# Attention, routing and MoE items on one core: a lent PSUM bank, a third sum on VectorE, the last pair in another order, and three kinds of step a slot later

## The chip, the cores and the metric

The kernel runs on one core of a Trainium2 chip. The time is the device time of one launch in microseconds; the figure that counts is the median of some runs, and beside it stands one execution that the hardware profiler recorded. The core's engines are TensorE (PE in the rows, with its weight loads as PEld), VectorE (DVE), ScalarE (ACT), GpSimd (POOL) and SyncE (SP, which issues most transfers). PSUM, where TensorE puts its results, has eight banks.

## The reference, cut to what matters

Three layers follow one another: attention with a tanh cap, a gated MoE that sends each token to its best expert, and a soft MoE whose experts work on 4 slots each.

```python
# 4 batches, 12 heads, 448 tokens, head size 64
scores = cap * np.tanh(scale * (q @ k.T) / cap)
attn = np.exp(scores - max); attn /= attn.sum(-1) + 1e-9
x = attn @ v                            # to (1792 tokens, 768)

# gated MoE: 8 experts, 768 -> 1024 -> 768
e_idx = argmax(x @ w_gate + modality_bias[modality_id], 1)
gate_w = softmax(logits)[e_idx]
out[e_idx == e] = gate_w * (relu(x @ w1[e]) @ w2[e])

# soft MoE: 8 experts, 4 slots each
logits = out @ phi
slot_input = softmax(logits, over tokens).T @ out
slot_out[e] = relu(slot_input[e] @ w1[e]) @ w2[e]
return softmax(logits, over slots) @ slot_out
```

## The kernel before, in words

**What sets the order.** The schedule is written by hand: each engine runs its instructions in the order in which the code issues them, and only semaphores hold it back. So an instruction that waits holds all that stands behind it on its engine. The table P near the end of the file (lines 1468 to 1475) gives the slots of the later part; nothing is planned at run time.

**Attention** works on 24 pairs of heads, 6 for each batch (NP_), as a pipeline. In the loop over p, TensorE makes the scores of pair p in three pieces (scores1, scores2, scores3), adds the products with v of pair p-1 (pv, then the last small piece pv2), and turns and normalises pair p-2 (post2, post3). The 448 keys are 3 chunks of 128 and a rest of 64; the rests of the pair's two heads share one 128-row tile. ScalarE takes tanh and exp, VectorE splits q and k into high and low parts (split), adds the exponentials of the chunks (adds1, adds2, 128x896 each) and scales the results. The sums over keys come from TensorE in post2 (line 507): each term of `sums[p]` is a tile under a constant weight `onesel`, in four column blocks, and a further term under the gate's weights `wg` gives the MoE logits. A pair has three such terms, head 0, head 1 and the shared rest.

**Banks in attention.** The pool ps_s has the tags s (two banks), s1, s2 and s0, ps_o and ps_x have one bank each, and ps_m has one, with tag "sm". In "sm" lie r_ps (the sums, read by VectorE at line 110), rt_ps (their transpose), and everything of the routing: rank_ps, tab_ps, tabt_ps. Tag s0 is used once a pair, by the second head of chunk 2 (scores3).

**Routing** of a batch begins two pairs after its last pair. The list `later` holds its steps, and the loop pops one at two places of each pair, once after post2 and once after scores3: s0 (9 small VectorE steps, the best expert), s1 (rank_ps: two matmuls that count tokens ahead of each one, then four additions to `base` and one for `rk`), s2, s3. After the third batch route_first follows: the most frequent expert, its slot table a2f, the sums over it (tab_ps, 12 small matmuls, line 329), their turn (tabt_ps, line 336), the indices, the gather of 4 tiles of rows by GpSimd (line 470) and the first expert weights. The fourth batch is routed later, in the item A.

**The last pair** (p = 23, LAST) goes through the same loop body. Then item_start closes the pools of attention and opens those of the items; the first weights are split (wsplits), ScalarE scales the four gathered tiles (xscale with True, line 478), and the last products and post steps follow, with six pieces that transpose and split the gathered rows (xpreps, line 766) between them.

**The items.** An item is one expert over 4 tiles of 117 gathered tokens, in 16 slots of 9 accumulating matmuls (128x468, lines 822 to 824: high times high, low times high, high times low). Item A comes first, then items 0, 1 and 2. `std_slots` puts further work into the slots by P: "pa" and "pb" are the second layer's logits and transposes for one quarter of the hidden rows (l_ps, h_ps, and s_ps in the later items), "dq" and "wq" quarters of 256 columns that are turned into q_ps and copied by VectorE to dhT and wphi (line 813), "comb" the combine weights of the item before (c_ps, line 862, a transpose of mcur into a bank of the Turns pool, which q_ps also uses). "plan" in A holds the routing of the fourth batch. At the end of an item the rows of the next are scaled and turned (xp, xprep). A rarely taken branch lies between A and item 0 (line 1219); after item 2 come the closing slots and the soft MoE, about 405 to 499 us, which stream their weights.

Of the kernel before, what the change touches and what calls it, by code (L numbers as in the profile page):

```python
# [9 lines left out]
F32 = mybir.dt.float32  # L10
# [42 lines left out]
def attn_moe_softmoe(ctx, tc, qT, kT, vP, cap, modality, w_gate, mod_bias, w1, w2, w2t, phi, m2_w1, m2_w2, out):  # L53
# [18 lines left out]
    W = 117  # L72
# [247 lines left out]

    def slot_tables(n, cols, col, sp, pp):
# [12 lines left out]
        def turn():  # L334
            tp = pp.tile([W, 2, NTAB], F32, tag="sm", name="tabt_ps")
            nc.tensor.matmul(tp.rearrange("p a n -> p (a n)"), lhsT=hold["sb"], rhs=fold, start=True, stop=True)
            tables(tp[:, :, :n], n, col, sp)

        return [sums, turn]
# [17 lines left out]

    def route_first(sp, pp):

# [33 lines left out]

        return [s0, s1, rest] + slot_tables(NT, NC1, NA, sp, pp)

# [171 lines left out]
    def attention(a1, a1q, a2p, first, ps_s, ps_o, ps_x, ps_m, item_start):  # L567
# [65 lines left out]

        def pv(p):
            vt = raw[p][2]
            o = o_t[p] = ps_o.tile([128, S], F32, tag="o", name="o_ps")
            for c in range(NKC):
                for h in range(2):
                    hd = slice(HD * h, HD * h + HD)
                    nc.tensor.matmul(o[hd], lhsT=vt[:, c, hd], rhs=pt_t[p][:, c, h] if c < 2 else pt_m[p][:, 1 + h],  # L640
                                     start=(c == 0), stop=False)
# [10 lines left out]
        extra.update({5 + i: call(nc.vector.memset, xg[:, i], 0.0) for i in range(NT)})  # L652
        extra[9] = zero_c
        n2 = 0
        spl[0] = first_split
        later = []
        for p in range(NPAIR):
            if p + 2 < NPAIR:
                raw[p + 2] = load_qkv(a1, a1q, p + 2)
            if p >= 4 and p % 2 == 0 and n2 < NRING + 1:  # L660
                m2_load(n2)
                n2 += 1
            scores1(p)
            if p >= 1:
                pv(p - 1)
                adds2(p - 1)
            if p + 1 < NPAIR:
                split(p + 1)
            if p >= 2:
                post2(p - 2, a1, ps_x, ps_m)  # L670
            if later:
                later.pop(0)()
            if p >= 1:
# [8 lines left out]
            if p in extra:  # L682
                extra[p]()
            if later:
                later.pop(0)()
            if p >= 2 and (p - 2) % NP_ == NP_ - 1:
                b = (p - 2) // NP_
                rb = route_batch(b, a2p, ps_m)
                later += rb
                if b == NB1 - 1:  # L690
                    f = route_first(a2p, ps_m)
                    later[-2] = lambda: (rb[-2](), f[0]())
                    later += [f[1], lambda: (f[3](), f[2]()), lambda: (f[-1](), gather(NA, NB1 * S), weights_first()),
                              lambda: None, lambda: None]
                later.pop(0)()
        while later:
            later.pop(0)()
        assert n2 == NRING + 1 and a1.end <= UNIT * (NRINGA - 1)
        wsplits, xpreps = item_start()
        wsplits[0]()  # L700
        xscale(NA, True)
        pv(LAST)
        adds2(LAST)
        post2(LAST - 1, a1, ps_x, ps_m)
        wsplits[1]()
        for f in xpreps[:3]:
# [241 lines left out]
    def std_slots(first, last, ncol, col, it, final=False):  # L948
# [8 lines left out]
        prep_x = lambda k: call(xprep, k, ("x", "sm", "sm")[k % 3])  # L957
        if not last:
            for k in range(3, KD):
                at(HB - 1, prep_x(k))  # L960
# [39 lines left out]
        fd, fw = quarters("dacc", "dhT", False), quarters("wacc", "wphi", first)  # L1000
        if not first:
            at(0, call(post_a, NF - 1))
            at(p["la"], logits_a)
# [107 lines left out]
    def prologue(key, e, col, rows=None, further=True):  # L1111
# [8 lines left out]
        for j in range(NR2):  # L1120
            w2load(j, e)
        for k in range(KD):
            xprep(k, "xa"[k % 2])

    def attention_any_cap():

        with ExitStack() as st:
# [12 lines left out]
            for p in range(NPAIR):  # L1140
# [43 lines left out]
                if hp == NP_ - 1:  # L1184
                    for f in route_batch(b, gx, ps_m):
                        f()
                    if b == NB1 - 1:
                        for f in route_first(gx, ps_m):
                            f()
# [80 lines left out]
    with ExitStack() as st:  # L1270
# [199 lines left out]
    "A": {"T": [0, 0, 0, 0, 3, 3, 3, 3], "wm": 3, "wq": 5, "pa": [6, 6, 9, 9, 12, 12, 15], "pb": [6, 7, 9, 10, 12, 13, 15], "nt": [10, 12, 12, 12], "cur": 10, "xp": [14, 14,  # L1470
        14], "xs": [13, 13, 13, 13], "plan": [0, 1, 1, 2, 2, 3, 4, 5, 7, 8, 8, 8, 9], "pool": [2, 3, 4, 6, 7, 8, 10, 14, 15]},
    "B": {"la": 0, "lb": 0, "lc": 5, "dturn": 1, "dh": 4, "dq": 5, "T": [0, 0, 0, 0, 4, 4, 4, 4], "wm": 4, "wq": 5, "pa": [6, 6, 9, 9, 12, 12,
        15], "pb": [6, 7, 9, 10, 12, 13, 15], "N": [6, 6, 6, 9, 9, 9, 9, 12], "comb": 5, "gath": 0, "cur": 12, "xp": [13, 13, 13], "xs": [1, 4, 4, 12], "rest": [1, 3, 7,
        9], "pool": [4, 5]},
# [69 lines left out]
```

## Time and profile before

| | before |
|---|---|
| median of 3 runs | 511.52 us (510.08 to 512.67) |
| the profiled execution | 508.24 us, its span 506.5 us |
| PE busy | 459.2 us, 91% of the span |
| DVE, ACT, POOL busy | 276.3, 250.3, 68.6 us |
| moved by DMA | 124.98 MB, mean 247 GB/s |
| attention | 0 to about 206 us |
| item A | 208.4 to 257.9 us |
| items 0, 1, 2 | 257.9 to about 405 us |
| closing slots, soft MoE | about 405 to 499 us |

The profiled execution is read by its stages, since each has another limit. A view by stretches gives the busy time of each engine, TensorE's granted clock (1.00 is 2.4 GHz, 0.50 is 1.2 GHz) and the share of the DMA engines. A timeline gives each instruction with the idle time of its engine before it and what ended that. A view of waits adds up what an engine waited for, line by line.

### The profile page before, as it was taken

How to read it: one execution, taken by the hardware profiler on the slowest of the kernel's cores; microseconds unless marked ns; L12 is line 12 of the kernel's file. 1: busy time of each engine (PE TensorE's matmuls, PEld its weight loads, DVE VectorE, ACT ScalarE, POOL GpSimd, SP SyncE). 2: the span in 40 equal slices, each digit the busy share in tenths (PEclk: the TensorE clock that was granted, in tenths of full speed). 3: DMA queues.
4: the chain of work that ended last, by engine and by line, in shares of the span. 5: the costliest groups of instructions: out<-in, count | busy, mean ns of one | idle time of the engine just before them, and what ended most of it. 6: DMA issues, size and time to landing. Idle time of an engine off the chain costs nothing. (4 is left out here: it accounts for less than half of the span.)

```text
span 506.5 us, 10871 instructions
## 1 busy us (share of the span) xinstructions
PE 459.2 (91%) x4181; PEld 298.6 (59%) x4181; DVE 276.3 (55%) x710; ACT 250.3 (49%) x402; POOL 68.6 (14%) x141
## 2 busy tenths in 40 slices
PE   7999989999999978989988999899989979977672
PEld 4556555564655544668875888688868845521221
DVE  4779889788978884575752355235523322001323
ACT  4988868787788767433442344234432311100222
POOL 3000000000000004024331403140014003120000
PEclk8999999999999999999999999999999989995987
DMA  6356644744353408679959797979589899999997
GB/s 198 103 119 189 219 140 124 230 138 114 121 157 104 132 20 226 209 260 356 283 170 338 217 319 233 325 234 313 200 295 326 292 393 415 416 411 417 414 414 285
DMA packets 56151, 124.98 MB, mean 247 GB/s; under 512 B 9385, under 2 KB 25456, under 8 KB 56096
## 3 DMA queue, kind: packets, MB, share of 16 engines
q1 hardware_dynamic: 53696, 117.54, 67.6%
q0 software_dynamic: 2256, 6.71, 4.7%
q8 instruction: 34, 0.56, 0.4%
q14 instruction: 21, 0.17, 0.1%
q10 hardware_dynamic: 144, 0.00, 0.0%
HBM read 112.52 MB, written 11.71 MB: 245 GB/s over the span
## 5 line engine op out<-in xcount | busy, mean ns | idle before, releaser
L608 ACT ACTIVATE arena<-arena,capb 128x1792 f32<-128x1792 f32 (+1 forms) x48 | 77.0, 1604 | 1.6
L822 PE MATMUL acc_ps<-xh,wh 128*128 128x468 f32 x192 | 75.7, 394 | 1.4 <-DVEq L1219 1.3
L107 DVE TENSOR_TENSOR wl<-rw,wh 128x384 fp32r<-128x384 f32 x49 | 27.4, 559 | 87.4 <-ACT wh L775 76.1
L823 PE MATMUL acc_ps<-xl,wh 128*128 128x468 f32 x192 | 71.9, 375 | 0.0
L824 PE MATMUL acc_ps<-xh,wl 128*128 128x468 f32 x192 | 71.7, 374 | 0.0
L107 DVE TENSOR_TENSOR arena<-arena 128x896 f32<-128x896 f32 x48 | 52.2, 1088 | 24.5 <-ACT arena L608 22.4
L640 PE MATMUL o_ps<-arena 128*64 128x448 f32 x288 | 59.6, 548 | 1.1 <-issue 0.5
L775 ACT CAST wh<-rw 128x384 fp32r<-128x384 f32 x64 | 32.5, 508 | 52.3 <-PE acc_ps L823 32.3
L605 ACT ACTIVATE arena<-s_ps 128x448 f32<-128x448 f32 x96 | 46.8, 541 | 8.6 <-PE s_ps L577 8.6
L470 POOL DMA_INDIRECT xg<-x_dram,idx x16 | 17.4, 1091 | 205.7 <-PE s_ps L577 176.6
L822 PEld LDWEIGHTS acc_ps<-xh,wh 128*128 128x128 f32 x192 | 36.1, 188 | 7.3 <-ACTq L1219 1.5
L943 ACT ACTIVATE h<-acc_ps 128x468 f32<-128x468 f32 x32 | 18.0, 562 | 43.0 <-PE acc_ps L824 40.5
L824 PEld LDWEIGHTS acc_ps<-xh,wl 128*128 128x128 f32 x192 | 36.0, 188 | 4.7 <-DVE wl L107 0.2
L823 PEld LDWEIGHTS acc_ps<-xl,wh 128*128 128x128 f32 x192 | 36.3, 189 | 3.5
L640 PEld LDWEIGHTS o_ps<-arena 128*64 128x64 f32 x288 | 18.5, 136 | 31.3 <-issue 21.7
L577 PE MATMUL s_ps<-qh,kh 64*128 64x448 f32 x144 | 31.9, 439 | 1.3 <-ACT kh L730 0.9
L600 ACT ACTIVATE arena<-sl_ps 128x448 f32<-128x448 f32 x24 | 13.1, 544 | 28.8 <-PE sl_ps L577 25.6
L577 PE MATMUL s_ps<-qh,kl 64*128 64x448 f32 x144 | 26.7, 366 | 0.1
L577 PE MATMUL s_ps<-ql,kh 64*128 64x448 f32 x144 | 26.7, 366 | 0.0
L107 POOL TENSOR_TENSOR wl<-rw,wh 128x384 fp32r<-128x384 f32 x15 | 15.4, 1026 | 75.6 <-ACT wh L775 41.2
L871 POOL DMA_INDIRECT c_dram<-cw,icur x16 | 17.5, 1094 | 51.1 <-DVE cw L107 34.4
L577 PEld LDWEIGHTS s_ps<-qh,kh 64*128 64x128 f32 x144 | 13.7, 187 | 17.1 <-ACT arena L605 8.5
(271 smaller groups left out, 759.0 us busy)
## 6 DMA issues: line engine op xcount, KB each, us to landing
ring<-in_moe_w_dram SPq DMA_DIRECT2D x30, 768.0 KB
w2r<-in_moe_w2t_dram SPq DMA_DIRECT2D x32, 384.0 KB
w2r<-in_moe_w_dram SPq DMA_DIRECT2D x28, 384.0 KB
arena<-in_moe_w_dram SPq DMA_DIRECT2D x13, 768.0 KB
rw<-in_moe_w_dram SPq DMA_DIRECT2D x24, 384.0 KB
arena<-in_moe_w_dram SPq DMA_DIRECT2D x22, 384.0 KB
arena<-in_v_dram SPq DMA_DIRECT2D x24, 256.0 KB
kr<-in_k_dram SPq DMA_DIRECT2D x23, 256.0 KB
```

The costliest lines, as they stand in the source:

```text
L107: (eng or nc.vector).tensor_tensor(out=out, in0=in0, in1=in1, op=op)
L470: nc.gpsimd.indirect_dma_start(out=xg[:, i, :], out_offset=None, in_=x_dram if rows is None else x_dram[:rows], in_offset=bass.IndirectOff ...
L577: nc.tensor.matmul(o, lhsT=kk[r, k], rhs=qq[r], start=(t == 0), stop=(t == 2))
L605: nc.scalar.activation(out=dst[:, h], in_=ps[h], func=AF.Tanh)
L608: nc.scalar.activation(out=t, in_=t, func=AF.Exp, scale=capb)
L640: nc.tensor.matmul(o[hd], lhsT=vt[:, c, hd], rhs=pt_t[p][:, c, h] if c < 2 else pt_m[p][:, 1 + h], start=(c == 0), stop=False)
L775: nc.scalar.copy(wh, rw)
L822: nc.tensor.matmul(ps, lhsT=wh, rhs=hi[k], start=(k == 0), stop=False)
L823: nc.tensor.matmul(ps, lhsT=wh, rhs=lo[k], start=False, stop=False)
L824: nc.tensor.matmul(ps, lhsT=wl, rhs=hi[k], start=False, stop=(k == total - 1))
L871: nc.gpsimd.indirect_dma_start(out=c_dram[i % NCD], out_offset=bass.IndirectOffsetOnAxis(ap=icur[:, i:i + 1], axis=0), in_=cw[:, i, :], in ...
L943: nc.scalar.activation(out=big["h"][n % NHB], in_=acc.pop(n), func=AF.Relu)
```

## The change

- A class `Lent` hands out tag s0 of ps_s. In attention rank_ps, tab_ps and tabt_ps are put there in place of "sm"; r_ps and rt_ps keep "sm".
- The list `later` becomes a table `todo` of (pair, place), place 0 after scores1, 1 after post2, 2 after scores3. The steps s0 to s3 keep their places. tab_ps moves from pair 22's place 1 to its place 0, the turn with gather and first weights from place 2 to place 1 of pair 22.
- `fold_rest`: for 13 pairs ("quiet": p = 2, 3, 4, 6, 7, 10 to 13, 16 to 19) VectorE adds the shared rest of pair p-2 into the sums of its two heads, in two additions of 64 rows by 448, just ahead of adds2. The third term of post2 falls away for these: 8 of TensorE's 24 passes under onesel, as the trace counts them.
- The last pair has an order of its own: scores2 and scores3 come before post1 and post2 of the pairs ahead; post3(21) stands before the last chunk of pv(23); ScalarE scales tiles 1 and 3 of the gathered rows and VectorE tiles 0 and 2.
- P: in A's plan s1 and s2 of the fourth batch go from slot 2 to slot 3, s3 and the first step of what follows from 3 to 4; "comb" goes from 5 to 6.
- Pieces 3 to 5 of item 0's rows are turned in item 0's slot 0, no longer at the end of A; the rare branch's prologue makes three pieces instead of six.

```diff
-        def turn():
-            tp = pp.tile([W, 2, NTAB], F32, tag="sm", name="tabt_ps")
+            tp = (pt or pp).tile([W, 2, NTAB], F32, tag="sm", name="tabt_ps")
...
+        def fold_rest(p):
+
+            for (_, t), h in zip(sums[p][:2], range(2)):
+                r = slice(KL * h, KL * h + KL)
+                tt(t[r], t[r], pt_m[p][r, 0], ALU.add)
+            sums[p].pop()
+
-        def pv(p):
+        def pv(p, between=lambda: None):
...
+                if c == NKC - 1:
+                    between()
...
+        class Lent:
+
+            @staticmethod
+            def tile(shape, dt, tag, name):
+                n = math.prod(shape[1:])
+                a = "abcd"[:len(shape) - 1]
+                t = ps_s.tile([128, 512], dt, tag="s0", name=name)[:shape[0], :n]
+                return t.rearrange(f"p ({' '.join(a)}) -> p {' '.join(a)}", **dict(zip(a, shape[1:])))
+
+        todo = {}
+
+        def plan(b):
+
+            p, rb = (b + 1) * NP_ + 1, route_batch(b, a2p, Lent)
+            at = [(p, 2), (p + 1, 1), (p + 1, 2), (p + 2, 1)]
+            if b == NB1 - 1:
+                f0, f1, rest, sums_, turn = route_first(a2p, ps_m, Lent)
+                rb += [f0, f1, sums_, rest, lambda: (turn(), gather(NA, NB1 * S), weights_first())]
+                at += [(p + 1, 2), (p + 2, 2), (p + 3, 0), (p + 3, 0), (p + 3, 1)]
...
+        quiet = set(range(2, LAST - 3)) - {5} - {(b + 1) * NP_ + 2 + i for b in range(NB1) for i in range(2)}
...
             scores1(p)
+            route(p, 0)
+            if p in quiet:
+                fold_rest(p - 2)
             if p >= 1:
                 pv(p - 1)
                 adds2(p - 1)
-            if p + 1 < NPAIR:
-                split(p + 1)
+            if p == LAST:
+                scores2(p)
+                adds1(p)
+                scores3(p)
+                pv2(p - 1)
+                post1(p - 1)
+                post2(p - 2, a1, ps_x, ps_m)
+                break
+            split(p + 1)
...
         wsplits, xpreps = item_start()
-        wsplits[0]()
-        xscale(NA, True)
-        pv(LAST)
+        pv(LAST, lambda: post3(LAST - 2, a1, ps_m))
+        for i in range(NT):
+            xscale(NA, bool(i % 2), i)
         adds2(LAST)
         post2(LAST - 1, a1, ps_x, ps_m)
-        wsplits[1]()
+        for f in wsplits:
+            f()
...
-        if not last:
-            for k in range(3, KD):
+        if not last and not first:
+            for k in range(KD // 2, KD):
                 at(HB - 1, prep_x(k))
...
         if not first:
+            if it == 0:
+                for k in range(KD // 2, KD):
+                    at(0, prep_x(k))
             at(0, call(post_a, NF - 1))
...
-        for k in range(KD):
+        for k in range(KD if further else KD // 2):
             xprep(k, "xa"[k % 2])
...
-    "A": ... "plan": [0, 1, 1, 2, 2, 3, 4, 5, 7, 8, 8, 8, 9]
+    "A": ... "plan": [0, 1, 1, 3, 3, 4, 4, 5, 7, 8, 8, 8, 9]
-    "B": ... "comb": 5
+    "B": ... "comb": 6
```

How the order moves. **First place: TensorE in pair 22**, from the products with v (o_ps, 64x448) of pair 21 on; the brackets name the engine or queue whose semaphore an instruction waits for. Before:

```order
L640 MATMUL o_ps<-arena 64x448 [waits DMAHW6_49,DVE_49]
L640 MATMUL o_ps<-arena 64x448 x3
L640 MATMUL o_ps<-arena 64x448 [waits Activation_49]
L640 MATMUL o_ps<-arena 64x448
L507 MATMUL r_ps<-arena,onesel 32x112 [waits DVE_49,PE_49]
L507 MATMUL r_ps<-arena,onesel 32x112 x11
L507 MATMUL r_ps<-arena,wg 32x112 x4
L514 MATMUL x_ps<-ident,arena 112x128 [waits DVE_49]
L514 MATMUL x_ps<-ident,arena 112x128 x3
L329 MATMUL tab_ps<-bsel,a_104 32x117 [waits DVE_49]
L329 MATMUL tab_ps<-bsel,a_104 32x117 x11
L644 MATMUL o_ps<-arena 128x448
```

After, from the same pair's table sums on (lines in attention are some 9 higher):

```order
L329 MATMUL tab_ps<-bsel,a_104 32x117 [waits DVE_49,PE_49]
L329 MATMUL tab_ps<-bsel,a_104 32x117 x11
L649 MATMUL o_ps<-arena 64x448 [waits DMAHW6_49]
L649 MATMUL o_ps<-arena 64x448 x3
L649 MATMUL o_ps<-arena 64x448 [waits Activation_49]
L649 MATMUL o_ps<-arena 64x448
L507 MATMUL r_ps<-arena,onesel 32x112 [waits DVE_49]
L507 MATMUL r_ps<-arena,onesel 32x112 x11
L507 MATMUL r_ps<-arena,wg 32x112 x4
L514 MATMUL x_ps<-ident,arena 112x128 x4
L336 MATMUL tabt_ps<-fold,tab 117x32
L653 MATMUL o_ps<-arena 128x448
```

The table's sums (tab_ps) have moved from behind x_ps to ahead of the products with v, and the turn (tabt_ps), which stood further down behind scores3, now stands right behind x_ps. The wait for VectorE that the products with v had is now at the table's sums.

**Second place: VectorE in a pair with a fold**, from the copy of o_ps (post1) to the k split of the next pair. Before:

```order
L648 COPY arena<-o_ps 128x448 [waits PE_49]
L522 RECIPROCAL arena<-rt_ps 112x8 [waits PE_49]
L107 TENSOR_TENSOR tmpg<-rt_ps,arena 112x4x2x8 [waits DVE_49]
L107 TENSOR_TENSOR arena<-x_ps,arena 112x512 [waits DMAHW3_49]
L107 TENSOR_TENSOR arena<-arena 128x896 [waits Activation_49]
L732 CAST kh<-kr 128x512 [waits DMAHW0_49,PE_49]
```

After, from the reciprocal on:

```order
L522 RECIPROCAL arena<-rt_ps 112x8 [waits PE_49]
L107 TENSOR_TENSOR tmpg<-rt_ps,arena 112x4x2x8 [waits DVE_49]
L107 TENSOR_TENSOR arena<-x_ps,arena 112x512 [waits DMAHW7_49]
L107 TENSOR_TENSOR arena<-arena 64x448 x2
L107 TENSOR_TENSOR arena<-arena 128x896 [waits Activation_49]
L767 CAST kh<-kr 128x512 [waits DMAHW4_49,PE_49]
```

Two additions of 64x448, without a wait of their own, now stand between the scaling of x_ps and the addition 128x896 (adds2) that waits for ScalarE's exp.

**Third place: TensorE in item 0, the end of slot 4 and slot 5.** q_ps is the turn of the dispatch quarter (htok) and of the phi quarter (wmid), c_ps the turn for the combine weights. Before:

```order
L812 MATMUL q_ps<-ident,wmid 128x128 [waits Activation_49]
L812 MATMUL q_ps<-ident,wmid 128x128
L862 MATMUL c_ps<-ident,mcur 117x128 [waits DVE_49]
L822 MATMUL acc_ps<-xh_2486,wh_2488 128x468
L823 MATMUL acc_ps<-xl_2487,wh_2488 128x468
L824 MATMUL acc_ps<-xh_2486,wl_2489 128x468
```

After, at q_ps:

```order
L847 MATMUL q_ps<-ident,wmid 128x128 [waits Activation_49]
L847 MATMUL q_ps<-ident,wmid 128x128
L857 MATMUL acc_ps<-xh_2454,wh_2456 128x468
L858 MATMUL acc_ps<-xl_2455,wh_2456 128x468
L859 MATMUL acc_ps<-xh_2454,wl_2457 128x468 [waits DVE_49]
```

and nine acc_ps matmuls further on, between slots 5 and 6:

```order
L864 MATMUL l_ps<-h_2462,wphi 32x117 [waits DVE_49]
L864 MATMUL l_ps<-h_2462,wphi 32x117 x3
L864 MATMUL l_ps<-h_2463,wphi 32x117 x4
L925 MATMUL s_ps<-w2r_2466,dhT 32x192 [waits DMAHW5_49,PE_49]
L925 MATMUL s_ps<-w2r_2466,dhT 32x192 x3
L925 MATMUL s_ps<-w2r_2467,dhT 32x192 [waits DMAHW6_49]
L925 MATMUL s_ps<-w2r_2467,dhT 32x192 x3
L925 MATMUL s_ps<-w2r_2468,dhT 32x192 [waits DMAHW7_49]
L925 MATMUL s_ps<-w2r_2468,dhT 32x192 x3
L870 MATMUL h_ps<-ident,h_2462 117x128 x4
L897 MATMUL c_ps<-ident,mcur 117x128 [waits PE_49]
L857 MATMUL acc_ps<-xh_2460,wh_2458 128x468 [waits Activation_49]
```

c_ps has left its place right behind q_ps, and stands behind slot 6's l_ps, s_ps and h_ps.

## Rows read from the trace of the kernel before

**Rows 1.** Busy time by stretches: attention, an item, the end; PEclk, DMA share, GB/s.

```profile
50.00:60.00 10.00, 9.96 (x90) 5.50 (x88) 8.07 (x15) 8.69 (x12) 0.00 (x0) 1.00 0.59 192
...
310.00:330.00 20.00, 18.27 (x153) 13.50 (x152) 7.95 (x27) 5.69 (x15) 4.60 (x5) 1.00 0.98 307
...
404.00:444.00 40.00, 36.45 (x538) 19.86 (x536) 8.35 (x41) 6.57 (x18) 7.66 (x20) 0.96 1.00 407
```

**Rows 2.** Waits of PE, whole span: in total, times, longest.

```profile
PE c_ps L862 <- DVE dhT L813: 5.2, 3, 1.7
...
PE rank_ps L285 <- DVE arena L110: 3.2, 3, 1.7
...
PE rank_ps L285 <- DVE ex L107: 2.1, 1, 2.1
PE tab_ps L329 <- DVE arena L110: 1.7, 1, 1.7
...
PE acc_ps L822 <- DVEq L1219: 1.3, 1, 1.3
```

**Rows 3.** Timeline, 52 to 62 us, pair 5: start, duration, engine, operation [idle before].

```profile
53.73 0.78 PE L507 MATMUL r_ps<-arena,onesel 128*32 128x112 f32 x24
...
54.33 0.38 PE L507 MATMUL r_ps<-arena,wg 128*32 128x112 f32 x8
...
58.58 0.70 DVE L236 MEMSET xg<- 117x768 f32 x1
...
60.05 1.09 DVE L107 TENSOR_TENSOR arena<-arena 128x896 f32<-128x896 f32 x1 [0.78 <-ACT arena L608]
...
61.40 0.78 PE L507 MATMUL r_ps<-arena,onesel 128*32 128x112 f32 x24
```

**Rows 4.** VectorE's groups by shape: times, busy, mean ns, idle before.

```profile
L107 DVE TENSOR_TENSOR arena<-arena 128x896 f32<-128x896 f32 x48 | 52.2, 1088 | 24.5 <-ACT arena L608 22.4
L107 DVE TENSOR_TENSOR wl<-rw,wh 128x384 fp32r<-128x384 f32 x49 | 27.4, 559 | 87.4 <-ACT wh L775 76.1 <-PE h_ps L835 5.8 <-PE xt_ps L766 2.3
...
L110 DVE TENSOR_SCALAR xg<-xg,gsl 117x768 f32<-117x768 f32 x12 | 7.8, 662 | 2.0 <-DMA xg<-x_dram,idx 1.9
```

**Rows 5.** Timeline, pair 8: the rank counts and VectorE behind them.

```profile
72.30 0.35 PE L285 MATMUL rank_ps<-oh,tri 112*112 112x32 f32 x2 [1.66 <-DVE arena L110]
...
73.56 0.18 DVE L107 TENSOR_TENSOR rk<-rank_ps,base 112x32 f32<-112x32 f32 x1
```

**Rows 6.** Timeline, pair 22: products with v, the slot table, its sums, their turn.

```profile
179.76 2.48 PE L640 MATMUL o_ps<-arena 128*64 128x448 f32 x12
...
181.86 0.20 DVE L107 TENSOR_TENSOR a<-f_am,gate 112x48 f32<-112x48 f32 x1
...
185.38 0.81 PE L329 MATMUL tab_ps<-bsel,a 112*32 112x117 f32 x24 [1.67 <-DVE arena L110]
...
189.48 0.36 PE L336 MATMUL tabt_ps<-fold,tab 128*117 128x32 f32 x2 [0.81 <-DVE tmpg L107]
```

**Rows 7.** Timeline, last pair: gather, sums and their read, scaling, first item matmul.

```profile
191.41 1.88 POOL L470 DMA_INDIRECT xg<-x_dram,idx  x1 [176.58 <-PE s_ps L577]
...
194.18 0.38 PE L507 MATMUL r_ps<-arena,wg 128*32 128x112 f32 x8
...
197.07 0.33 DVE L110 TENSOR_SCALAR arena<-r_ps,gvec 128x112 f32<-128x112 f32 x1 [4.81 <-PE sl_ps L577]
...
201.35 3.41 ACT L478 ACTIVATE xg<-xg,gsl 117x768 f32<-117x768 f32 x4
...
208.41 0.48 PE L822 MATMUL acc_ps<-xh,wh 128*128 128x468 f32 x1
```

**Rows 8.** Stretches of 2 us after the items: the granted clock falls, returns.

```profile
408.00:410.00 2.00, 1.26 (x9) 0.78 (x13) 1.28 (x5) 0.67 (x3) 0.00 (x0) 0.80 1.04 433
410.00:412.00 2.00, 2.00 (x24) 0.95 (x20) 0.00 (x0) 0.00 (x0) 0.00 (x0) 0.50 1.01 421
412.00:414.00 2.00, 1.45 (x18) 0.43 (x10) 0.00 (x0) 0.37 (x1) 0.00 (x0) 0.84 1.01 424
```

More of the change, by code (lines that the diff above doesn't have):

```diff
@@ L319, in tables, with slot_tables @@
         nc.vector.tensor_copy(gsl[:, col:col + n], tb[:, 1, :])
-    def slot_tables(n, cols, col, sp, pp):
+    def slot_tables(n, cols, col, sp, pp, pt=None):
         hold = {}
@@ L356, in rest_tables, with route_first @@
         tables(tp, n, NTAB, sp)
-    def route_first(sp, pp):
+    def route_first(sp, pp, pt):
         hold = {}
@@ L392, in s1 @@
                 tt(a2f[:, :NC1, i, :NT], am, val[:, :NC1].unsqueeze(2).to_broadcast([C, NC1, NT]), ALU.mult)
-        return [s0, s1, rest] + slot_tables(NT, NC1, NA, sp, pp)
+        return [s0, s1, rest] + slot_tables(NT, NC1, NA, sp, pp, pt)
     def route_final(sp, pp):
@@ L653, in attention, with route @@
         extra[9] = zero_c
+        class Lent:
[13 more added lines that the diff above has]
+                at += [(p + 1, 2), (p + 2, 2), (p + 3, 0), (p + 3, 0), (p + 3, 1)]
+                assert p + 4 == LAST
+            for k, f in zip(at, rb, strict=True):
+                todo.setdefault(k, []).append(f)
+        def route(p, place):
+            for f in todo.pop((p, place), ()):
+                f()
+        quiet = set(range(2, LAST - 3)) - {5} - {(b + 1) * NP_ + 2 + i for b in range(NB1) for i in range(2)}
         n2 = 0
         spl[0] = first_split
-        later = []
         for p in range(NPAIR):
@@ L666, in attention @@
                 adds2(p - 1)
-            if p + 1 < NPAIR:
-                split(p + 1)
+            if p == LAST:
[7 more added lines that the diff above has]
+            split(p + 1)
             if p >= 2:
                 post2(p - 2, a1, ps_x, ps_m)
-            if later:
-                later.pop(0)()
+            route(p, 1)
             if p >= 1:
@@ L683, in attention @@
                 extra[p]()
-            if later:
-                later.pop(0)()
             if p >= 2 and (p - 2) % NP_ == NP_ - 1:
[L687 to L698, printed above, removed]
+                plan((p - 2) // NP_)
+            route(p, 2)
+        assert not todo and n2 == NRING + 1 and a1.end <= UNIT * (NRINGA - 1)
         wsplits, xpreps = item_start()
-        wsplits[0]()
-        xscale(NA, True)
-        pv(LAST)
+        pv(LAST, lambda: post3(LAST - 2, a1, ps_m))
+        for i in range(NT):
+            xscale(NA, bool(i % 2), i)
         adds2(LAST)
         post2(LAST - 1, a1, ps_x, ps_m)
-        wsplits[1]()
+        for f in wsplits:
+            f()
         for f in xpreps[:3]:
@@ L1187, in attention_any_cap @@
                     if b == NB1 - 1:
-                        for f in route_first(gx, ps_m):
+                        for f in route_first(gx, ps_m, ps_m):
                             f()
@@ L1470 @@
     "A": {"T": [0, 0, 0, 0, 3, 3, 3, 3], "wm": 3, "wq": 5, "pa": [6, 6, 9, 9, 12, 12, 15], "pb": [6, 7, 9, 10, 12, 13, 15], "nt": [10, 12, 12, 12], "cur": 10, "xp": [14, 14,
-        14], "xs": [13, 13, 13, 13], "plan": [0, 1, 1, 2, 2, 3, 4, 5, 7, 8, 8, 8, 9], "pool": [2, 3, 4, 6, 7, 8, 10, 14, 15]},
+        14], "xs": [13, 13, 13, 13], "plan": [0, 1, 1, 3, 3, 4, 4, 5, 7, 8, 8, 8, 9], "pool": [2, 3, 4, 6, 7, 8, 10, 14, 15]},
     "B": {"la": 0, "lb": 0, "lc": 5, "dturn": 1, "dh": 4, "dq": 5, "T": [0, 0, 0, 0, 4, 4, 4, 4], "wm": 4, "wq": 5, "pa": [6, 6, 9, 9, 12, 12,
-        15], "pb": [6, 7, 9, 10, 12, 13, 15], "N": [6, 6, 6, 9, 9, 9, 9, 12], "comb": 5, "gath": 0, "cur": 12, "xp": [13, 13, 13], "xs": [1, 4, 4, 12], "rest": [1, 3, 7,
+        15], "pb": [6, 7, 9, 10, 12, 13, 15], "N": [6, 6, 6, 9, 9, 9, 9, 12], "comb": 6, "gath": 0, "cur": 12, "xp": [13, 13, 13], "xs": [1, 4, 4, 12], "rest": [1, 3, 7,
         9], "pool": [4, 5]},
```

## The prediction

> **What bounds the kernel now.** I read the view by stretches first. In attention TensorE is busy 9.96 of 10 us at a granted clock of 1.00, and VectorE 8.07; in the items TensorE is busy 18.27 of 20, with the DMA engines at 0.98; from 404 us on the DMA share is 1.00 [rows 1]. So up to about 404 us TensorE's queue sets the time, and there is to be won what it idles and what it computes too often. The last stage is set by its transfers, but they start as the items free their places, so a gain ahead of it counts, unless transfers already hold the items.
>
> The second view is the sum of TensorE's waits. Five of its lines are touched by this change: three c_ps for 5.2, three rank counts for 3.2 (the longest 1.7), a fourth rank count for 2.1, the table's sums for 1.7, and the first matmul of item 0 for 1.3 [rows 2]. That is 13.5 us, the upper end for moved waits. The third view is the timeline of single pairs, for what ends each wait. All durations are of the profiled execution, 508.24 us; the median of the runs, 511.52, is 3.28 above it, and I carry the differences over to the median as they are.
>
> **Folding the third sum.** In a steady pair the sums begin at 53.73 and at 61.40, a period of 7.67; the 24 passes of the three terms take 53.73 to 54.33, which is 0.60, so 8 passes are 0.20 [rows 3]. Thirteen pairs lose them: at most -2.6. VectorE gets two additions of 64x448 for it, a shape that the trace does not have. By shape, 128x384 takes 0.56 and 128x896 takes 1.09 [rows 4]; a straight line between gives 0.62 for 448 columns, and 0.56 to 1.09 are the ends. VectorE's free time: it waits 0.78 for exp ahead of adds2 in a pair that also has a 0.70 memset [rows 3], so 1.48 without one. Two additions at 0.62, together 1.24, fit into 1.48; TensorE and ScalarE cover them. I count 10 pairs at -0.20. In pairs 6 and 7 the memset takes 0.70 of that, and 10 and 16 follow a rank pair with VectorE late; I count pairs 7, 10 and 16 at +0.15 each, for an addition that ends behind its exp. Sum -1.55, between -2.6 and, with 1.09 each, the slower rival below.
>
> **The lent bank.** In pair 8 the rank counts wait 1.66 [rows 5], because rank_ps shares a bank with r_ps, which VectorE reads late, behind the nine steps of s0. In bank s0 nothing is left of that wait. But TensorE's next use of s0 is the second head of chunk 2, and that now waits until VectorE has read the counts, at 73.56 plus 0.18 [rows 5]. In pair 8 VectorE comes late: pairs 5 to 8 have a memset each, 1.24 less 0.78 leaves 0.46 over in each of pairs 6 and 7, so 0.92. From 1.66 there remain 0.74, and I take off 0.3 for the second head: -0.45. The other two counts wait (3.2 - 1.7)/2, 0.75 each [rows 2]; no memset is there, and I take -0.75 each. Sum -1.95, between 0 and -3.2.
>
> **The table in pair 22.** Before, TensorE reaches the products with v at 179.76, and the sums wait 1.67 for the same bank at 185.38, the turn 0.81 at 189.48 [rows 6]. After, the sums stand ahead of the products and need a2f, whose last step begins at 181.86 and lasts 0.20 [rows 6]. That is 2.3 us behind 179.76, some 2.9 behind the time at which TensorE would get there with its earlier gains. 1.67 and 0.81 go, 2.3 to 2.9 come: I count 0, between -1.0 and +1.0. What is won is only the turn's place: the indices and the gather come about 3 us earlier.
>
> **The late read beside the gather.** GpSimd issues the gather from 191.41 on. The sums of the pair in work end at 194.18 + 0.38 = 194.56, and VectorE, which had been idle for 4.81, reads them at 197.07 [rows 7]: 2.5 us with nothing else in the trace to explain them. An earlier gather falls on other steps of pairs 22 and 23. If it delays nothing that TensorE needs, part of the 2.5 is won; if it meets two such reads, as much again is lost. I count +0.8, between -2.5 and +2.5.
>
> **The last pair.** ScalarE scales the four tiles from 201.35 in 3.41, 0.85 each, and the first item matmul is at 208.41 [rows 7], behind transposes and splits that need these tiles. Two of the four go to VectorE at 0.66 each [rows 4] and run beside, so the chain gets up to 1.7 shorter; the post steps that stood behind scores now run earlier under products with v. I count -1.5, between 0 and -2.5.
>
> **Item A, the border, the items.** The fourth rank count waits 2.1 for VectorE's `ex` [rows 2]; a slot later, with 9 matmuls more in front, that wait is covered but for some 0.3 (an estimate, for the chain of small steps behind it): -1.8, between -1.0 and -2.1. At the border the wait of 1.3 [rows 2] is for VectorE's splits of the next rows. Three pieces of transposes and splits go to item 0's slot 0: the same passes on TensorE, in front of matmuls that need them later. The first matmul may still wait for the logits of A's last quarter: -0.1, between -0.6 and +0.5. In each of three items c_ps waits for VectorE's copy dhT, 5.2/3 = 1.73 each [rows 2], since both lie in one bank's rotation; behind slot 6's other work this copy is long done, and the 9 matmuls of slot 5, with both splits ready, run under it. The combine weights come a slot later, but their first use as dispatch lies in the next item, and VectorE is busy under half there. -1.65 each, -4.9 in all, between 0 (a rival) and -5.2.
>
> **The sum.** -1.55 - 1.95 + 0 + 0.8 - 1.5 - 1.8 - 0.1 - 4.9 = -11.0. From 508.24 that is 497.2 for a profiled execution, and from the median of 511.52 it is 500.5.
>
> **The rivals.** *Transfers hold the items.* From 310 to 330 the DMA share is 0.98 [rows 1]; if the weights' transfers already set the pace there, each item only turns the wait for dhT into one for weights. For it speaks that share; against it that the waits of c_ps are ended by VectorE [rows 2]. Then the 4.9 go: 500.5 + 4.9 = 505.4.
>
> *The gather's delay moves along.* It falls on a read that TensorE waits for, +2.5 in place of +0.8, and the border gives back 0.5: 502.7.
>
> *VectorE is overfilled.* Its free 1.48 fills to 1.24, and any lateness passes from pair to pair. The folds and the lent bank then bring nothing: 500.5 + 1.55 + 1.95 = 504.0.
>
> *The banks do not part what they should.* The wait for r_ps returns at the second head of chunk 2, and the table's stall in pair 22 costs its upper end: +1.95 + 1.0, and 503.5.
>
> *Slower: the additions of 64 rows are dear.* VectorE works 7.67 - 1.48 = 6.19 us a pair. With two additions at a each it sets the pace as soon as 6.19 + 2a is over the new 7.47, at a = 0.64. At 1.09 [rows 4] a pair takes 8.37, 0.70 more than before, 9.1 in 13 pairs, while -7.5 of the other terms stay (without folds and lent bank): 511.52 + 1.6 = 513.1. At twice my estimate, 1.24 each, it is 8.67, so 13.0 - 7.5 = +5.5 and 517.0. It decides from a = 1.03. Against it speaks that VectorE's rows grow with columns, not with rows [rows 4].
>
> *The clock falls in pair 22.* The trace has one fall of the granted clock behind the items, beside idle time of TensorE (1.26 busy of 2 us): 0.80, 0.50 and 0.84 in three stretches of 2 us [rows 8], which costs 0.40 + 1.00 + 0.32 = 1.7. A stall of 2.9 in front of the table's sums could do the same; the wait of 2.1 in item A [rows 2] lies in a stage that stayed at full clock. Then 502.2. The Trainium skill (TensorE: Matmul & The Clock Gate, Part 1, What's actually happening) puts it as "the default state is throttled, and activity releases the throttle"; by that rule a new idle stretch costs more than its length, and rows 8 agree with it, 0.50 being 1.2 GHz.
>
> **How the numbers follow.** Chances: the forecast, within 3 us of 500.5, 0.53; transfers 0.13; the gather 0.11; VectorE overfilled 0.07; the banks 0.05; the clock 0.07; dear additions 0.04 (half of them within 0.5%). The predicted time is the forecast's, 500.5. Below 497 and above 506 lie the dear additions and the tails of the sum, not quite 2 in 10; so the range is 497 to 506. A measurement of this kernel can tell about 0.5%, 2.6 us, from no change: 508.9 and 514.1 are the bounds. All cases but the dear additions lie under 508.9, and I leave some room for two rivals at once: faster 0.91, same 0.06, slower 0.03.
>
> **What would show it.** Right: no wait of rank counts for line 110 and none of c_ps for dhT; 16 passes under onesel in 13 pairs and a period of 7.47 in pairs 11 to 13; TensorE idle for 2 to 3 us in front of tab_ps; the first item matmul about 204.2 in place of 208.41; the last stage as long as before and 11 us earlier. Wrong: a 64x448 addition over 0.64, sums that wait for VectorE in quiet pairs, waits for weights in the items in place of those for dhT, a granted clock under 1.00 between 180 and 210, or a last stage that begins earlier and ends as before.

## The result: about 1% faster, half of what was forecast

Over 16 runs of each kernel the changed one takes 505.02 us in the median (502.82 to 510.43), the kernel before 510.08 (507.28 to 515.15). The ratio, without the few runs that lie over 1.5% above the fastest of their kernel, is 0.989, with a 95% interval of 0.9867 to 0.9912. The forecast of 500.5 lay 4.5 us lower; the range of 497 to 506 holds the time. The profiled execution takes 503.55 with a span of 501.8, against 508.24 and 506.5.

### The profile page after: what moved, and what is told of

It is laid out like the page before. It is cut to its first block, busy times and chain, and to the rows that moved or that the text cites. A ratio compares the mean times of both kernels' runs of the same rounds, so it can differ in the third digit from the quotient of the medians.

```text
span 501.8 us, 10684 instructions
## 1 busy us (share of the span) xinstructions
PE 461.4 (92%) x4077; PEld 298.2 (59%) x4077; DVE 291.0 (58%) x738; ACT 248.7 (50%) x400; POOL 66.7 (13%) x141
## 5 line engine op out<-in xcount | busy, mean ns | idle before, releaser
L107 DVE TENSOR_TENSOR arena<-arena 128x896 f32<-128x896 f32 (+1 forms) x74 | 68.0, 919 | 13.2 <-ACT arena L608 11.4
L649 PE MATMUL o_ps<-arena 128*64 128x448 f32 x288 | 61.9, 565 | 0.4 <-DVE arena L657 0.3
L906 POOL DMA_INDIRECT c_dram<-cw,icur x16 | 16.0, 1003 | 55.4 <-DVE cw L107 42.2
```

What stands on the lines that cost most here:

```text
L107: (eng or nc.vector).tensor_tensor(out=out, in0=in0, in1=in1, op=op)
```

## The profile after

To see where the time went I read the same landmarks out of both timelines: the start of ScalarE's tanh on sl_ps in a pair of attention, and the first matmul of an item's slot. All stretches below are differences of such starts; the last item matmul is the last of the kind high times high, and the last instruction counts by its end.

| stretch | before | after | measured | forecast |
|---|---|---|---|---|
| start to pair 2 | 25.97 | 27.08 | +1.1 | 0 |
| pair 2 to pair 21 | 151.30 | 147.60 | -3.7 | -3.5 |
| pair 21 to the first item matmul | 31.14 | 34.72 | +3.6 | -0.7 |
| from there to slot 13 of A | 38.42 | 37.13 | -1.3 | -1.8 |
| to slot 5 of item 0 | 27.54 | 28.40 | +0.9 | -0.1 |
| to the last item matmul | 129.72 | 125.79 | -3.9 | -4.9 |
| to the last instruction | 95.21 | 94.64 | -0.6 | 0 |

The sum is -3.9; the span differs by 0.8 more, behind the last instruction. More than half of what is missing, 4.3 of 7.1, is in one row, the passage from pair 21 to the items. There the changed kernel loses 3.6 where I had a small gain.

TensorE's waits of the changed kernel, in the form of [rows 2] (in total, times, longest):

```profile
PE tab_ps L329 <- DVE a L107: 2.8, 1, 2.8
PE xt_ps L801 <- ACT xg L478: 2.1, 1, 2.1
...
PE acc_ps L857 <- DVEq L1257: 0.9, 1, 0.9
PE s_ps L925 <- DMA w2r<-in_moe_w_dram: 0.8, 2, 0.5
```

No rank count waits any more and no c_ps, as forecast. The wait for the slot table is there with 2.8, as estimated. The wait for a gathered tile (xt_ps turns it, ScalarE scales it first) has grown from 0.7 to 2.1, and new is 0.8 for w2r in the items. The timeline of pair 22, to be read beside [rows 6]:

```profile
179.83 1.40 PE L329 MATMUL tab_ps<-bsel,a 112*32 112x117 f32 x24 [2.77 <-DVE a L107]
181.16 4.75 PE L649 MATMUL o_ps<-arena 128*64 128x448 f32 x12
```

The same 12 passes that took 2.48 at 179.76 in [rows 6] take 4.75. The view by stretches says why (columns as in [rows 1]; the last three numbers are the granted clock, the DMA share and GB/s):

```profile
178.00:180.00 2.00, 0.17 (x4) 0.20 (x8) 1.55 (x8) 1.97 (x5) 0.00 (x0) 0.75 0.37 91
180.00:182.00 2.00, 2.00 (x28) 1.14 (x25) 0.64 (x5) 1.51 (x1) 0.00 (x0) 0.50 0.09 24
182.00:184.00 2.00, 2.00 (x8) 0.68 (x6) 1.97 (x6) 0.00 (x0) 0.00 (x0) 0.50 0.03 8
184.00:186.00 2.00, 2.00 (x14) 0.40 (x14) 1.39 (x3) 0.00 (x0) 0.00 (x0) 0.54 0.77 237
```

TensorE was busy 0.17 of 2 us, and then works at a granted clock of 0.50, which is 1.2 GHz, from 180 to nearly 186. That is the rival "the clock falls in pair 22", at nearly twice the price that I gave it, and one of the signs that I had named for being wrong. The second loss stands beside [rows 7]: the gather's last issue, the scaling of its tile, the turn that needs it, and the first item matmul.

```profile
193.32 1.09 POOL L470 DMA_INDIRECT xg<-x_dram,idx  x1 [0.30 <-issue]
...
203.93 0.94 ACT L478 ACTIVATE xg<-xg,gsl 117x768 f32<-117x768 f32 x1 [4.27 <-DMA xg<-x_dram,idx]
...
204.91 1.12 PE L801 MATMUL xt_ps<-ident,xg 117*128 117x117 f32 x9 [2.14 <-ACT xg L478]
...
209.40 0.61 PE L857 MATMUL acc_ps<-xh,wh 128*128 128x468 f32 x1
```

The gather starts 2.3 us earlier than in [rows 7], 189.09 against 191.41, and its last tile lands later, at 203.9 against 202.0. ScalarE waits 4.27 for it, TensorE 2.14, and the granted clock falls once more (0.58 and 0.57 from 206 to 210). SyncE's queue shows what is new beside the gather: four loads of w2r, 384 KB each.

```profile
191.24 1.94 SPq L824 DMA_DIRECT2D w2r<-in_moe_w2t_dram  x4
```

Before, they were issued at 200.46, behind a store that waited for post3 of pair 21:

```profile
199.93 0.33 SPq L528 DMA_DIRECT2D x_dram<-arena  x1
200.46 2.12 SPq L789 DMA_DIRECT2D w2r<-in_moe_w2t_dram  x4
```

In the new order of the last pair that post3 comes after item_start, so the loads pass the store and run beside the gather. Each ratio below is against the kernel before on the same chip; the changed kernel was not timed again beside them, so a ratio beside its 0.989 is a rougher comparison than a stretch of two profiles. The theory is: the stall lowers the clock, and the w2r loads hold back the gather. The rivals: pair 22's passes are slow for another reason, and the gather is slow wherever it runs.

## Experiments on the passage to the items

### The table's sums at their old place

```diff
-                at += [(p + 1, 2), (p + 2, 2), (p + 3, 0), (p + 3, 0), (p + 3, 1)]
+                at += [(p + 1, 2), (p + 2, 2), (p + 3, 1), (p + 3, 1), (p + 3, 2)]
```

> The changed kernel with one thing undone: the table's sums (tab_ps) stand behind x_ps of pair 22 again and the turn with the gather behind scores3; the lent bank stays. Theory (the 2.77 us stall ahead of tab_ps makes the granted clock fall to 0.50 for 6.8 us): the stall is under 0.5 us, the granted clock is 1.00 from 176 to 190, the 12 passes of o_ps take about 2.5 us and not 4.75, and the first item matmul comes 3 to 6 us earlier than 209.40; ratio to the kernel before about 0.980 (changed kernel 0.989). Rival (the table's place is not what costs; the earlier gather is worth as much): the first item matmul stays within 1 us of 209.40, ratio 0.988 to 0.992.

The clock stays at 1.00 from 176 to 190, and pair 21 to 22 takes 10.74 (14.32 in the changed kernel), though tab_ps waits 1.66 for the read of r_ps again, which I had put under 0.5. But from pair 23 to the first item matmul it takes 21.09 (13.67), since now the four tiles land 9.8 to 13.7 us after their issue, the clock is 0.63 over 200 to 214, and TensorE waits for the tiles:

```profile
PE xt_ps L801 <- ACT xg L478: 5.1, 2, 4.6
...
PE wphi_ps L834 <- DMA w2r<-in_moe_w2t_dram: 3.0, 4, 1.8
PE xt_ps L801 <- DVE xg L110: 2.6, 3, 1.8
```

Ratio 0.9928 (0.9889 to 0.9966). The first half of the theory held, the forecast of the time did not: the 3.6 us won in pair 22 went into the second loss, and 4.1 more. The profiled execution, 513.38, is the slowest of 12; by the ratios the kernel is 0.4% behind the changed one.

### The w2r loads behind the scaling

```diff
         for i in range(NT):
             xscale(NA, bool(i % 2), i)
+        for f in w2loads:
+            f()
...
-            for j in range(NR2):
-                w2load(j, e_first[-1])
```

> The changed kernel with the four w2r loads (384 KB each) issued behind the scaling of the gathered rows, no longer at the start of the items. Theory (these loads, now 9 us earlier, hold back the gather's last tile, which lands 10.58 us after its issue; before it was 5.60): the last tile lands by 201, TensorE's wait of 2.14 us for it is under 0.5, no granted clock of 0.50 between 200 and 212, first item matmul 2 to 3.5 us earlier than 209.40, ratio about 0.983. Rival (the gather is slow because it runs beside the other transfers, whatever their order): the tile lands at 203 to 204 as now, ratio 0.988 to 0.992.

The view by tile gives the time from a gather's issue to its landing (least, median, most); first the changed kernel, then this one:

```profile
DMA to landing us min/median/max: 9.6/10.1/10.6
```

```profile
DMA to landing us min/median/max: 4.4/5.1/5.4
```

The wait for the tile is gone, the clock does not fall between 200 and 214, and pair 23 to the first matmul takes 11.24, 2.4 less. Ratio 0.9776 (0.9714 to 0.9837). The loads were the cause of the late tile. In pair 22 the clock falls as before: 14.43.

### Both

The two diffs above in one kernel.

> Both edits together: sums and turn at their old places, w2r loads behind the scaling. Theory (two separate costs, both clock falls with them): granted clock 1.00 from 176 to 212, first item matmul at 203 to 204.5, ratio about 0.976 to 0.979. Rival (one cause with two faces): no better than the better of the two alone, ratio 0.980 to 0.984.

Pair 21 to the first item matmul takes 29.76, 5 us less than in the changed kernel, and the clock stays at 1.00 up to 447. In the passage both costs are separate. The ratio is only 0.9807 (0.9759 to 0.9854), in the range of the rival: the stretch from slot 13 of A to slot 5 of item 0 gives back 2.2 (30.59 for 28.40). And one wait of before has come back:

```profile
PE tab_ps L329 <- DVE arena L110: 1.7, 1, 1.7
```

### The stall filled with work

```diff
+            if p == LAST - 1:
+                dummy = Lent.tile([128, S], F32, "s0", "dummy")
+                for _ in range(13):
+                    nc.tensor.matmul(dummy, lhsT=spl[p][2][:, :KC], rhs=spl[p][0], start=True, stop=True)
             route(p, 0)
```

> The changed kernel with 13 more matmuls of 128x448 in front of the table's sums of pair 22, into the lent bank, whose result nobody reads: the stall is filled with work, its place and what it waits for stay. Theory (the idle time, and not the wait, makes the clock fall): granted clock 1.00 from 176 to 190, o_ps about 2.5 us for its 12 passes, sums of the table at the same 179.8, first item matmul 2 to 3.4 us earlier, ratio about 0.983. Rival (the passes behind the stall are slow for another reason, or the fall comes anyway): o_ps stays at 4.75, ratio 0.988 to 0.992 or above.

The filling and what stands behind it, in TensorE's timeline:

```profile
175.97 2.94 PE L703 MATMUL dummy<-qh,kh 128*128 128x448 f32 x13
178.84 0.81 PE L329 MATMUL tab_ps<-bsel,a 112*32 112x117 f32 x24
179.58 2.48 PE L649 MATMUL o_ps<-arena 128*64 128x448 f32 x12
```

With the same place and the same thing waited for, the passes take 2.48 again and the clock stays at 1.00. One such profile could be chance, since the stall is not always followed by a fall (see the end). But in the seven profiles that have only waits up to 1.7 there (the kernel before, old place, both, tab_ps lent) or have the stall filled (this one and two below) the clock is 1.00, and in four of the seven that have it the clock falls. So in these 14 profiles no fall comes without the stall's idle time, and the idle time does not bring one each time. Behind the late tile the clock still falls (0.88 over 200 to 214). Ratio 0.9748 (0.9689 to 0.9808).

### The bank of tab_ps

A reading of the diff has to be corrected here. I wrote that tab_ps is put into the lent bank; it isn't. `sums` still takes `pp`, the bank of r_ps, and only `turn` takes the new argument. With the sums at their old place the wait of 1.7 for that bank is therefore back. Lending it too, on top of the kernel with both edits:

```diff
-            ps = pp.tile([128, W], F32, tag="sm", name="tab_ps")
+            ps = (pt or pp).tile([128, W], F32, tag="sm", name="tab_ps")
```

> The kernel of the two edits together (sums and turn at their old places, w2r loads late), and tab_ps too in the lent bank; in the changed kernel only the turn and the rank counts lie there, tab_ps still shares a bank with r_ps. Theory (the 1.67 us wait of tab_ps for the read of r_ps, back in that kernel, is the shared bank alone): the wait is under 0.3, from the sl_ps tanh of pair 21 to the first item matmul 28.0 to 28.4 us (29.75 with both edits, 34.7 in the changed kernel), ratio 0.974 to 0.979. Rival (VectorE, not the bank, is late: the copy of tab_ps waits behind the k and q splits): the stretch stays at 29.5 or more.

The wait is gone, pair 21 to 22 takes 8.95 and the whole passage 28.04, the shortest of all. The ratio is 0.9755 (0.9713 to 0.9797), not clearly better than the 0.9807 before this step: TensorE waits 2.8 for w2r, 2.3 of it at once in item 0, and slot 0 to slot 5 of item 0 takes 20.01 (18.46 in the changed kernel). What the earlier start wins is in part lost at transfers.

### Filling and late loads

The diffs of the filling and of the late loads in one kernel.

> The changed kernel with the 13 filling matmuls in front of the table's sums and the w2r loads late. Theory (two causes that add: clock in pair 22, transfers at the gather): granted clock 1.00 from 176 to 212, from the sl_ps tanh of pair 21 to the first item matmul 29.0 to 29.8 us (32.4 with late loads alone, 32.6 with the fill alone), ratio 0.973 to 0.978. Rival (the gather, now ready, is waited for by nobody and the last pair's own order is the bound): 31.5 or more.

The passage takes 29.46, and the clock stays at 1.00 up to 397. This is the fastest kernel of those with several runs: median 497.07, ratio 0.9677 (0.9638 to 0.9716). Its ratio, and those of the late loads and of the filling, lie lower than the passages alone explain: 10.9, 5.8 and 7.2 us below 0.989, for passages shorter by 5.3, 2.3 and 2.1. Where the rest comes from is not shown.

## Experiments on the terms of the sum

Each kernel from here on has one execution, and only its stretches are read. Pair 2 to 21 is steady enough for that: it takes 147.5 to 147.7 in all eleven profiles that have the folds and the lent bank.

### No folds

```diff
-        quiet = set(range(2, LAST - 3)) - {5} - {(b + 1) * NP_ + 2 + i for b in range(NB1) for i in range(2)}
+        quiet = set()
```

> The changed kernel without fold_rest in any pair: TensorE makes the third sum in all pairs again, VectorE has 26 additions less. Measured from the sl_ps tanh of pair 2 to that of pair 21: 151.30 before, 147.60 in the changed kernel. Theory of the prediction (folds -1.55, lent bank -1.95): 149.2. Rival (the quiet pairs' 0.2 is given back at pairs 9, 11 and 17, where the changed kernel loses 0.87, 0.44 and 0.47, because VectorE is late): 147.3 to 148.0, and no loss at those three pairs.

Pair 2 to 21 takes 148.00: the folds are worth 0.4. The additions cost 0.61 each, where I estimated 0.62, by VectorE's groups of the changed kernel:

```profile
L107 DVE TENSOR_TENSOR arena<-arena 64x448 f32<-64x448 f32 x26 | 15.9, 611 | 0.4
```

Quiet pairs do run at 7.47 to 7.49 for 7.68. But pairs 9, 11 and 17, one to three pairs behind a rank pair, take 8.53, 8.11 and 8.13 with folds and 8.09, 7.67 and 7.68 without: three times 0.44 is given back, and 0.3 more in pair 8. Behind pairs 10 and 16, the late pairs that I had expected, it is three times what I took.

### The rank counts in the old bank

```diff
-            p, rb = (b + 1) * NP_ + 1, route_batch(b, a2p, Lent)
+            p, rb = (b + 1) * NP_ + 1, route_batch(b, a2p, ps_m)
```

> The changed kernel with the rank counts of the first three batches in the bank of r_ps again (the turn of the table stays in the lent bank). Measured from the sl_ps tanh of pair 2 to that of pair 21: 151.30 before, 147.60 in the changed kernel, 148.00 without the folds. Theory after the run without folds (the folds are worth 0.4, so the lent bank must be worth the rest of 3.7): 150.6 to 151.2, and TensorE waits again for line 110 at three rank counts. The prediction's own split (lent bank -1.95): 149.3 to 149.8.

Pair 2 to 21 takes 151.28, the time of the kernel before to 0.02. The waits, to be read beside [rows 2], have grown from 3.2 to 4.0:

```profile
PE rank_ps L285 <- DVE arena L110: 4.0, 3, 2.1
```

So the lent bank is worth 3.3 without folds (151.30 to 148.00), the folds alone nothing, and both together 3.7. The folds' passes were won and paid back at the shared bank, where VectorE's read of r_ps ends the longer waits.

### The combine weights at their old slot

```diff
-    "B": ... "comb": 6
+    "B": ... "comb": 5
```

> The changed kernel with the combine weights in slot 5 of the items again. Measured from the first matmul of slot 5 to that of slot 8 of items 0, 1 and 2: 10.86, 10.87, 10.86 before; 9.11, 9.26, 10.55 in the changed kernel. Theory (c_ps waited for dhT alone; in item 2 the w2r transfers take the gain): 10.8 to 10.9 in items 0 and 1, 10.8 to 11 in item 2, so the move is worth 1.6 to 1.75 twice and 0.3 once. Rival (item 2's transfers are late because the items ahead got shorter): item 2 back to 10.86 with no wait for w2r, and items 0 and 1 at 9.5 or less because something else moved.

Slot 5 to slot 8 takes 10.88, 10.85 and 11.08, and c_ps waits for dhT again. The move is worth 1.77 and 1.59 in items 0 and 1, 0.5 in item 2. In item 2 of the changed kernel the gain runs into w2r:

```profile
377.23 0.53 PE L925 MATMUL s_ps<-w2r,dhT 128*32 128x192 f32 x8 [0.35 <-DMA w2r<-in_moe_w_dram]
...
378.22 0.53 PE L925 MATMUL s_ps<-w2r,dhT 128*32 128x192 f32 x8 [0.45 <-DMA w2r<-in_moe_w_dram]
...
379.21 0.27 PE L897 MATMUL c_ps<-ident,mcur 128*117 128x128 f32 x1
```

With late loads, alone or with the filling, item 2 takes 9.44 and 9.50, so that wait is not fixed; it hangs on when the items' transfers were issued.

### The plan of item A as before

```diff
-    "A": ... "plan": [0, 1, 1, 3, 3, 4, 4, 5, 7, 8, 8, 8, 9]
+    "A": ... "plan": [0, 1, 1, 2, 2, 3, 4, 5, 7, 8, 8, 8, 9]
```

> The changed kernel with the fourth batch's rank counts at their old slots (2 and 3) of item A. Measured from A's first matmul to that of slot 13: 38.43 before, 37.13 in the changed kernel, and on to slot 5 of item 0: 65.96 before, 65.53 changed. Theory (the slot removes the wait of 2.1 for ex): 38.4 to 38.9 to slot 13, and the border no shorter, 65.5 to 67 to slot 5. Rival (A's end waits for the gather of item 0's rows, so what the slot wins is given back there): 38.4 to 38.9 to slot 13, but 65.3 to 65.9 to slot 5 as now.

The wait for `ex` is back with 2.09, and A takes 38.07 to slot 13 (37.13 in the changed kernel), 67.23 to slot 5 of item 0 (65.53). Slots 2 and 3, where the rank counts stand, take 8.15 against 6.72 in the changed kernel and 5.84 in four others (filled, no folds, filling with late loads, and the last one below). In the changed kernel slot 3's products with w2r take 2.31 up to the rank counts, 1.43 without folds, with a wait of 0.27 for w2r among them. So the slot is worth 1.4, and 2.3 where w2r has landed; the border does not give it back here, but it varies by more than that.

### Item 0's pieces at A's end

```diff
-        if not last and not first:
+        if not last:
             for k in range(KD // 2, KD):
                 at(HB - 1, prep_x(k))
...
-            if it == 0:
-                for k in range(KD // 2, KD):
-                    at(0, prep_x(k))
...
-        for k in range(KD if further else KD // 2):
+        for k in range(KD):
```

> The changed kernel with pieces 3 to 5 of item 0's rows turned at the end of item A again. Measured from the first matmul of slot 13 of A to that of slot 5 of item 0: 27.54 before, 28.40 in the changed kernel. Theory (the move costs: TensorE's 1.37 us of transposes and ScalarE's copies are only moved, and slot 3 of item 0 then waits 0.46 for ScalarE's wh): 27.4 to 27.8. Rival (the move is neutral, and the loss comes from the gather landing late in a shorter A): 28.2 to 28.6.

The border takes 28.23 (28.40). It takes between 27.7 and 30.7 in the other kernels, so the slots tell more. Before, slot 15 of A took 5.61 and slots 0 and 1 of item 0 together 6.17; in the changed kernel it is 3.97 and 7.65, and here 5.61 and 6.16: the move is worth 0.2, and the pieces are not what costs 0.9 there. That is 0.5 in slot 14 of A, which turns the gathered rows, 0.9 in slots 2 and 3 of item 0, with a wait of 0.46 for ScalarE's wh that only the changed kernel's profile has, less 0.4 in slot 4. The border's spread comes from slot 14 (3.1 to 5.8) and slot 4 of item 0 (5.6 to 8.5, with waits for w2r). The gathered tiles of item 0 land 5 to 12 us after their issue; none of the kernels changed that alone.

### The last pair in the old order

On top of the kernel with filling and late loads:

```diff
-            if p == LAST:
-                scores2(p)
...
-                break
-            split(p + 1)
+            if p + 1 < NPAIR:
+                split(p + 1)
...
-        pv(LAST, lambda: post3(LAST - 2, a1, ps_m))
-        for i in range(NT):
-            xscale(NA, bool(i % 2), i)
...
+        for f in w2loads:
+            f()
+        wsplits[0]()
+        xscale(NA, True)
+        pv(LAST)
...
```

> The kernel with fill and late w2r loads, but with the last pair in the old order (all four scalings on ScalarE behind scores3). Measured from the sl_ps tanh of pair 21 to the first item matmul: 29.46 with the new order, 31.14 in the kernel before. Theory (the new order is worth what the prediction gave it, 1.5): 30.8 to 31.3. Rival (with the gather landing early the scalings are covered in either order, and the gain was the gather's): 29.2 to 29.8.

The w2r loads stand ahead of the scaling again here, but behind the store of post3 of pair 21 as in the kernel before, and the tiles land 6.3 to 6.6 us after their issue. The passage takes 29.88 (29.46): the new order is worth 0.4, not 1.5. ScalarE's four scalings stand in a row again, and are nearly covered, since TensorE waits 0.23 and 0.50 for them:

```profile
197.16 3.41 ACT L478 ACTIVATE xg<-xg,gsl 117x768 f32<-117x768 f32 x4
```

## Why the prediction was right in sign and range, and twice too large

That the time lies in the range is in part luck: one loss had been counted at nothing and another as a rival at 0.07, and their sum stayed inside a range that was drawn for other reasons.

**Folds and lent bank.** The sum, -3.5, is what was measured, -3.7. For the split one step must be undone: at pair 8 I took 0.92 off the bank's gain for lateness that the folds bring. Counted with the folds, the forecast is -0.63 and -2.87; with the folds taken out first the runs show -0.4 and -3.3. Two prices were off. The late pairs 10 and 16 were put at +0.15 each, and 0.44 was lost behind each. And the bank won more than the waits: without folds the three pairs with rank counts are shorter by 1.91 (of which 0.58 come back in the next two pairs), 0.99 and 1.00, for waits of 1.66, 0.75 and 0.75.

**The table in pair 22.** The stall was sized rightly, 2.3 to 2.9 against 2.77, and the step "I count 0" held without the clock: in three profiles (no folds, old plan, old pieces) the stall stands as it is, the clock stays up, and pair 21 to 22 takes 11.25 to 11.47, with 6.75 for the next pair; that is 2.4 to 2.6 less than before over the two pairs. Of this 0.9 is the last pair's new order (with the old one pair 22 to 23 takes 7.66) and 1.0 the late read, so 0.5 to 0.7 is left. With the clock down pair 21 to 22 takes 12.90 and 13.06 (rank counts, combine weights) or 14.32 and 14.43 (the changed kernel, late loads). I had this as a rival at 0.07 and 1.7 us; the stall lowered the clock in 4 of the 7 profiles that have it, for about 1.5 to 3. The price failed because I took the fall of [rows 8] as the size of any fall; the same trace has a longer one, 0.85 and 0.64 in the two stretches of 10 us from 450 to 470.

**The late read beside the gather.** It was forecast at +0.8 for signals that arrive late. r_ps in the last pair is now read at once (VectorE idle for 0.18 where it was 4.81), and with it went a wait that TensorE had right behind that read in the kernel before:

```profile
197.46 0.32 PE L520 MATMUL rt_ps<-ident,arena 128*112 128x128 f32 x1 [0.96 <-issue]
```

So the read itself is worth about -1.0; but the gather's own landing became the bound. This is the step that failed outright: I costed the last pair's new order on ScalarE and VectorE, and did not follow SyncE's queue, where the w2r loads passed the store ahead of them. Late loads won 2.4 back at once, and more in the ratio. The passage closes from its parts: filled and with late loads it takes 29.46, 1.7 less than before, where I forecast 0.7 less; the clock in pair 22 adds 2.8 (14.32 for 11.51) and the loads beside the gather 2.4 (13.67 for 11.22), which makes the +3.6.

**The last pair** was mis-sized, -0.4 for -1.5. **Item A**: -1.3 for -1.8, since slot 3 gave 0.9 of the 2.3 back at w2r. **The items**: -3.9 for -4.9, with items 0 and 1 at their 1.6 to 1.8 and item 2 at 0.3, where the rival "transfers hold the items" came true in one item of three. **The border**: +0.9 for -0.1, of which the pieces are -0.2 and the rest stands in slots that vary from kernel to kernel. The start costs 1.1: TensorE's wait for ScalarE's kh there is 1.9 in place of 0.9, ahead of any edited instruction, and starts of the same code spread by more than that among the experiments (25.0 to 27.8).

## What to carry to other kernels

When a step is moved, follow every queue that it passes, SyncE's above all: loads that used to stand behind a waiting store set off earlier, and what they delay can be the one transfer that the next stage waits for. Two edits on the same wait must be costed together: the passes saved on TensorE were worth nothing until the bank that VectorE read late was parted. And a stall moved into one piece may cost more than its length, while the same idle time in another execution costs only itself.

## What was not expected of the hardware

The clock's answer to the same stall is not the same each time: with 2.5 to 2.8 us of idle time at the same place, four profiles show a clock below 1.00 behind it and three show 1.00. One of the three, the kernel with item 0's pieces at A's end:

```profile
178.00:180.00 2.00, 0.82 (x26) 0.68 (x28) 0.93 (x6) 1.97 (x4) 0.00 (x0) 1.00 0.46 115
180.00:182.00 2.00, 2.00 (x12) 0.68 (x12) 1.85 (x8) 0.90 (x1) 0.00 (x0) 1.00 0.03 8
```

The page of the Trainium skill that the prediction cites (TensorE: Matmul & The Clock Gate, Part 1, What's actually happening) says that the gate goes by how busy the engine has been lately, and calls the ramp at a kernel's start "run-variable"; these profiles show the same of a fall in mid kernel. A single profile of such a kernel therefore carries 3 us of chance in this place, and only ratios over several runs settle what an edit there is worth.

An indirect gather of 4 tiles landed 4.4 to 6.6 us after its issue in the six kernels in which 1.5 MB of other loads were issued behind it (the kernel before, late loads, both edits, tab_ps lent, filling with late loads, old order), and 7.1 to 13.7 in the eight with these loads beside it. The fall of the clock behind the items in [rows 8] is missing in the changed kernel's profile and there in others; the last stage took between 94.2 and 96.6 in all of them.
